# Attention plus feed-forward block: unpairing the last hidden chunk and retuning which engine takes which step

## The chip, the cores and the metric

The kernel runs on one core of a Trainium2 chip. A core has five engines with instruction streams of their own: TensorE (PE in the profile; its weight loads are listed apart as PEld), VectorE (DVE), ScalarE (ACT), GpSimd (POOL) and SyncE (SP), which here issues nearly all DMAs.[...] The metric is the device time of one execution in microseconds (us), lower is better. The time before is 734.32 us, the median of three runs (733.95 to 736.05).

## What is computed

The reference, cut to what matters (S = 2048 rows, D = 640, H = 32 query heads of 20, one shared key and value head, F = 1728):

```python
x  = A_x                                  # 1 x 2048 x 640, bf16
xn = (x - mean(x)) / sqrt(var(x) + 1e-5)
q  = (xn @ wq), split in 32 heads of 20;  k = xn @ wk;  v = xn @ wv
p  = softmax(q k^T / sqrt(20))            # 32 heads x 2048 x 2048
attention    = concat(p v) @ wo
feed_forward = silu(xn @ w1) @ w2         # 640 -> 1728 -> 640
out = x + attention + feed_forward
```

The costly part is the exponential of 32 x 2048 x 2048 scores, 134 million of them.

## The kernel before

The program is laid out by a list scheduler that runs when the kernel is built: every operation is given to an engine with a guessed duration, and the scheduler fixes each engine's order. On the chip an engine follows that order and waits where a semaphore has not come yet.

The scores are worked through in 128 units (4 chunks of 512 query columns x 32 heads), three units to a group, so 43 groups (the last holds two units). A group takes 16 steps, one for each 128 keys, so there are 688 steps. A step writes three PSUM banks of scores (S, one 512-column matmul for each unit). Then it has one of two shapes:

- In a **ScalarE step** one exponential of 128x1536 does all three banks.
- In a **VectorE step** ScalarE takes two banks (128x1024), and VectorE takes the third by integer arithmetic: it clips the score into an int16 (Z) whose bits are a coarse exponential. Two shifted copies of it, Y0 (VectorE) and Y1 (GpSimd), are read as well, so that the sum of three readings is an accurate exponential. The PV matmuls read all of them: Z and Y0 with the step itself, Y1 later, as a "third reading".

```python
def want_dve(self, t):                       # is step t a VectorE step?
    if t < DVE_FROM or ... or t % KT in KT_ACT:
        return False
    back = ...   # work that VectorE has in front of it, in the scheduler's us
    return back < DVE_TH
```

The PV matmuls of a step fill up to four column groups of 32 in one pass. A ScalarE step leaves one column group free and can carry a third reading in it; but the first step of a group cannot, because the fourth group has not been started there:

```python
        gd = self.group_dve[g]               # VectorE steps of this group so far
        pv.after = None if dv or nh < 3 or gd == 0 else thirds
...
    def emit_thirds(self, ts, first):        # (cut)
        for op, _ in self.pv_wait:           # ScalarE steps that can host a reading
            if seen and self.can_host(op) and ts:
                self.host(op, ts.pop())
        while len(self.thirds) >= 3 or (end and self.thirds):
            ...                              # the rest: passes of their own ("PT"), three readings each
```

After a group its sums (U) are copied to SBUF, turned by a DMA transpose, and normalised by GpSimd and VectorE. Behind the transpose of the first group stand the late weight loads on the same SyncE queue:

```python
    def norm_dma(self, g, rows):
        op = sc.dma("sp", lambda q: q.dma_start_transpose(self.UT[:, up, :, 0:rows], self.U[0:rows, up, :]), ...)
        if g == LATE_G:                      # group 0
            self.late_loads(("U", up))       # w2, wo, and a 1 MB fill of the query buffer
        ...                                  # GpSimd: two copies, two adds; VectorE: reciprocal; GpSimd: product
```

The feed-forward has 14 hidden chunks: 13 of 128 rows and one of 64. Each chunk of 512 columns gets 5 matmuls, a tanh on ScalarE and a product on VectorE (silu by way of tanh). The 64-row chunk is worked for two column chunks at once, in the two halves of the array's columns, with one tanh and one product over 128 partitions for both:

```python
    def h_job(self, c, fk, step):
        pair = fk == FC - 1
        ...
                for z in range(2):
                    ins = pe.matmul(self.bk(b, 0, QW, z * FLAST, (z + 1) * FLAST), self.w1[:, k, fk * P:fk * P + FLAST],
                                    self.xnT[:, k, (c + z) * QW:(c + z + 1) * QW], ..., tile_position=(0, z * FLAST))
        ...
            sc.new("act", t_act(QW), lambda a: a.activation(t, src, AF.Tanh, scale=0.5), ...)
            sc.new("dve", t_dve_ps(QW), lambda v: v.scalar_tensor_tensor(out=self.hT[0:rows, fk, :], ...), ...)
```

Jobs of the feed-forward's second half (14 matmuls of 320 columns for each of 32 output tiles, `out_job`) are put between the steps where the scheduler sees room. What is left when the last step is done runs in the tail, with the last attention output.

The prologue norms x (16 tiles): statistics by VectorE or ScalarE (`ACT_STATS` names ScalarE's tiles), an inverse square root for each batch of tiles (`BATCHES`, `NW_ENG`), the norm itself (`NORM_ENG`), and a transpose by DMA (`DT`) or TensorE. `PRO` is the order of TensorE's prologue jobs (t: transpose, k, q, v, d).

Of the kernel before, what the change touches and what calls it, by code (L numbers as in the profile page):

```python
# [14 lines left out]
P = 128  # L15
# [3 lines left out]
DC = 5  # L19
SLOT = 32  # L20
BANK = 512
QW = 512
# [5 lines left out]
FC = 14  # L28
FLAST = F - 13 * P
# [23 lines left out]
KT_ACT = (0,)  # L53
# [12 lines left out]
DVE_TH = 3.4  # L66
# [14 lines left out]
DT = (4, 5, 6, 9, 10, 11, 12, 13, 14, 15)  # L81
NORM_P = 4.5
DVE_FROM = 8
PRO = "v0 t7 t8 v1 k2 k3 k4 q1 v2 d0 k5 k6 k7 v3"
ACT_STATS = (4, 6, 9, 12, 14)
NW_ENG = ("dve", "dve", "dve")
NORM_ENG = ("pool", "pool", "pool", "pool", "act", "pool", "act", "act", "dve", "act", "act", "act")
BATCHES = ((0, 4), (4, 10), (10, 16))
# [256 lines left out]
class Job:  # L345
    def __init__(self, name, mms, reads, consume, gate=None, min_step=-1, banks=None, on_start=None, width=0, hold=None, use=None, n=1):
        self.name = name
        self.mms = mms
        self.reads = reads
        self.consume = consume  # L350
        self.gate = gate
        self.min_step = min_step
        self.on_start = on_start
        self.begun = False
        self.width = width
        self.hold = hold
        self.use = use
        self.n = n


class Builder:
# [371 lines left out]
    def do_mm(self, job, now, d):  # L733
        work, fn = job.mms.pop(0)
        job.begun = True
        b = job.bank
        op = self.sc.new("pe", d, lambda pe: fn(pe, b), job.reads, [("B", b)], name=job.name, queue=False)
        op.mm = job.n
# [353 lines left out]
    def h_job(self, c, fk, step):  # L1092
        sc = self.sc
        rows = P
        pair = fk == FC - 1
        mms = []
        for k in range(DC):
            def f(pe, b, k=k):
                if not pair:
                    return pe.matmul(self.bk(b), self.w1[:, k, fk * P:(fk + 1) * P], self.xnT[:, k, c * QW:(c + 1) * QW],  # L1100
                                     start=(k == 0), stop=(k == DC - 1))
                for z in range(2):
                    ins = pe.matmul(self.bk(b, 0, QW, z * FLAST, (z + 1) * FLAST), self.w1[:, k, fk * P:fk * P + FLAST],
                                    self.xnT[:, k, (c + z) * QW:(c + z + 1) * QW], start=(k == 0), stop=(k == DC - 1),
                                    tile_position=(0, z * FLAST), skip_group_check=True)
                return ins
            mms.append((t_mm(QW), f))
# [13 lines left out]
        reads = [("xnT", 4 * c + i) for i in range(8 if pair else 4)] + [("w1",)]  # L1121
        return Job(f"h{c}_{fk}", mms, reads, consume, min_step=step, width=0 if pair else QW, n=2 if pair else 1)
# [32 lines left out]
    def out_job(self, c, i, e, step=-1, ffn=True, ks=range(DC), src="xres", dst="ost", hmax=H):  # L1155
# [6 lines left out]
        if ffn:  # L1162
            for fk in range(FC):
                r0 = FLAST * (c % 2) if fk == FC - 1 else 0
                r1 = r0 + FLAST if fk == FC - 1 else P

                def f(pe, b, fk=fk, r0=r0, r1=r1, m=len(mms)):
                    return pe.matmul(self.bk(b, 0, 320), self.hT[r0:r1, fk, i * P:(i + 1) * P],  # L1168
                                     self.w2[r0:r1, fk, e0:e0 + 320], start=(m == 0), stop=(m == tot - 1))
                mms.append((t_mm(320), f))  # L1170
# [78 lines left out]
    def fill_chunk(self, c, t):  # L1249
# [11 lines left out]
        hs = [(3.0, lambda s, fk=fk: self.h_job(c, fk, s)) for fk in range(FC) if fk < FC - 1 or c % 2 == 0]  # L1261
# [46 lines left out]
    def prologue(self):  # L1308
# [41 lines left out]
        for fk in range(FC):  # L1350
            rows = P if fk < FC - 1 else FLAST
            for r0 in ((0,) if rows == P else (0, FLAST)):
                w2p.append(lambda q, fk=fk, rows=rows, r0=r0: q.dma_start(self.w2[r0:r0 + rows, fk, :],
                                                                          self.B_w2[fk * P:fk * P + rows, :]))
# [325 lines left out]
```

## Time and profile before

| | |
|---|---|
| median of three runs | 734.32 us |
| span of the profiled execution | 732.1 us |
| TensorE busy | 714.9 us (98%) |
| ScalarE busy | 695.8 us (95%) |
| VectorE busy | 652.6 us (89%) |
| GpSimd busy | 524.8 us (72%) |
| exponentials of 128x1536 / 128x1024 / 128x512 | 49 / 625 / 14 |
| tanh of 128x512 | 54 |
| VectorE steps | 637 of 688 |

The profile has one line for each group of like instructions: line of the kernel, engine, operation, what is written and read, the count, busy time and mean ns, and after the second bar how long the engine had stood idle before them and what ended the idle time. L776 is the score matmul, L794 the exponential, L808 VectorE's clip, L878 its Y0, L814 GpSimd's Y1, L866 all PV matmuls, L1100 and L1103 the hidden layer, L1113 tanh, L1118 the product, L1168 the feed-forward's second half, L956/L953/L958/L972 GpSimd's normalisation, L699/L712/L693 matmuls of zeros that fill gaps.

Engine time is counted as the union of intervals, and matmul and ScalarE intervals overlap their successors a little. So the distance from one start to the next, read from the timeline, is a better price for one more instruction than its duration.

### The profile page before, as it was taken

To read this page: it belongs to the slowest core of one execution; us is meant where nothing else is said; L and a number is where in the kernel's file an instruction comes from. 1 tells how busy PE (TensorE), PEld (TensorE's weight loads), DVE (VectorE), ACT (ScalarE), POOL (GpSimd) and SP (SyncE) were. 2 spreads that over 40 slices of the span, in tenths; PEclk is the share of its full clock that TensorE was granted. 3 is DMA by queue.
4 is the path that set the end of the run, shared out by engine and by line. 5 is a ranking of instruction groups with operands and counts; after the bars stand their busy time and mean duration, and the time that the engine had idled before them with its cause. 6 is when DMAs were issued, how large, how long until landed. Compare 5 with 4: busy or idle time off the path is not lost.

```text
span 732.1 us, 18886 instructions
## 1 busy us (share of the span) xinstructions
PE 714.9 (98%) x6863; PEld 229.2 (31%) x6863; DVE 652.6 (89%) x1189; ACT 695.8 (95%) x780; POOL 524.8 (72%) x897
## 2 busy tenths in 40 slices
PE   8898999999999999999999999999999999999998
PEld 4432222223333233222333233222233322322335
DVE  7788898998998999999899999999989899999883
ACT  6999999999999999999999999999999999999960
POOL 4376877677787777777777777767778877776770
PEclk9999999999999999999999999999999999999999
DMA  9546000000003011000102011110002001200011
GB/s 273 148 123 190 15 17 17 21 15 17 23 9 44 9 52 52 21 18 17 9 8 52 9 26 46 40 19 23 14 8 45 9 9 34 62 9 8 9 38 37
DMA packets 58546, 29.22 MB, mean 40 GB/s; under 512 B 44406, under 2 KB 57814, under 8 KB 58454
## 3 DMA queue, kind: packets, MB, share of 16 engines
q1 hardware_dynamic: 56998, 27.79, 15.1%
q8 instruction: 56, 0.92, 0.6%
q10 hardware_dynamic: 1456, 0.22, 0.2%
q14 instruction: 36, 0.29, 0.1%
HBM read 11.44 MB, written 2.62 MB: 19 GB/s over the span
## 4 chain that ended last, share of the span: by engine, by line
PE 70%; ACT 20%; issue 5%; DVE 4%; DMA 1%; POOL 1%; DVEq 0%; ACTq 0%; POOLq 0%
PE psall L866 23%; PE psall L776 22%; ACT sbt L794 18%; PE psall L1168 8%; PE psall L1100 7%; PE psall L1173 2%; PE psall L1064 2%; PE psall L712 2%; ACT sbt L1113 1%; DVE sbt L808 1%; PE psall L699 1%; DMA sbt<-sbt 1%; DVE sbt L1118 1%; ACT sbt L1458 1%; DVE sbt L1438 0%
## 5 line engine op out<-in xcount | busy, mean ns | idle before, releaser
L794 ACT ACTIVATE sbt<-psall 128x1024 bf16<-128x1024 f32 (+2 forms) x688 | 661.9, 1110 | 9.2 <-PE psall L776 7.7
L814 POOL TENSOR_TENSOR sbt<-sbt 128x256 int32<-128x256 int32 x637 | 436.8, 692 | 158.6 <-DVE sbt L808 143.9
L808 DVE TENSOR_SCALAR sbt<-psall 128x512 int16<-128x512 f32 x637 | 425.9, 684 | 48.2 <-PE psall L776 43.3
L776 PE MATMUL psall<-sbt 32*128 32x512 bf16 x2048 | 269.6, 385 | 6.4 <-ACT sbt L794 3.3
L866 PE MATMUL psall<-sbt 128*32 128x512 bf16 x3534 | 269.2, 385 | 2.1 <-POOL sbt L814 2.1
L776 PEld LDWEIGHTS psall<-sbt 32*128 32x128 bf16 x2048 | 69.2, 91 | 246.8 <-ACT sbt L794 81.1
L878 DVE TENSOR_SCALAR sbt<-sbt 128x1536 int16<-128x1536 int16 (+1 forms) x218 | 132.0, 608 | 2.0
L866 PEld LDWEIGHTS psall<-sbt 128*32 128x32 bf16 x3534 | 66.8, 94 | 113.7 <-issue 77.6
L1168 PE MATMUL psall<-sbt 128*128 128x320 bf16 x448 | 85.4, 302 | 0.2 <-DVE sbt L1118 0.2
L1100 PE MATMUL psall<-sbt 128*128 128x512 bf16 x260 | 79.9, 384 | 2.2 <-DVE sbt L1118 1.9
L1168 PEld LDWEIGHTS psall<-sbt 128*128 128x128 bf16 x448 | 34.7, 97 | 43.7 <-issue 33.1
L1118 DVE SCALAR_TENSOR_TENSOR sbt<-sbt,psall 128x512 bf16<-128x512 bf16 x54 | 36.8, 682 | 2.3 <-ACT sbt L1113 0.7
L1113 ACT ACTIVATE sbt<-psall 128x512 bf16<-128x512 f32 x54 | 37.1, 687 | 0.0
L986 DVE CAST sbt<-psall 128x512 bf16<-128x512 f32 x43 | 29.3, 682 | 1.7 <-PE psall L866 1.6
L1100 PEld LDWEIGHTS psall<-sbt 128*128 128x128 bf16 x260 | 17.8, 97 | 40.7 <-issue 25.8
L1064 PE MATMUL psall<-sbt 128*128 128x512 bf16 (+1 forms) x95 | 29.2, 385 | 0.4 <-DVE sbt L1118 0.4
L1173 PE MATMUL psall<-sbt 128*128 128x320 bf16 x144 | 29.0, 303 | 0.5 <-issue 0.4
L972 POOL TENSOR_TENSOR sbt<-sbt 128x240 bf16<-128x240 f32 (+2 forms) x44 | 25.4, 578 | 2.3 <-DMA sbt<-sbt 1.4
L958 POOL TENSOR_TENSOR sbt<-sbt 128x44 f32<-128x44 f32 x84 | 26.0, 309 | 1.1
L956 POOL CAST sbt<-sbt 128x168 f32<-128x168 bf16 x42 | 14.1, 335 | 9.0 <-DMA sbt<-sbt 9.0
L712 PE MATMUL psall<-sbt 128*128 128x512 bf16 (+1 forms) x70 | 17.4, 403 | 1.9 <-POOL sbt L1368 1.5
L1185 DVE SCALAR_TENSOR_TENSOR sbt<-psall,sbt 128x320 bf16<-128x320 f32 x28 | 13.6, 486 | 6.1 <-PE psall L1168 5.9
(88 smaller groups left out, 207.9 us busy)
## 6 DMA issues: line engine op xcount, KB each, us to landing
sbt<-in_A_x_dram SPq DMA_DIRECT2D x32, 160.0 KB, 3.3
out_dram<-sbt SPq DMA_DIRECT2D x15, 160.0 KB, 1.8
sbt<-in_B_w_dram SPq DMA_DIRECT2D x5, 432.0 KB, 6.6
sbt<-sbt SPq DMA_DIRECT2D x105, 20.0 KB
sbt<-in_B_w_dram SPq DMA_DIRECT2D x13, 160.0 KB, 2.9
sbt<-sbt SPq DMA_TRANSPOSE x68, 2.4
sbt<-sbt SPq DMA_DIRECT2D x1, 1024.0 KB, 6.1
sbt<-in_A_wo_dram SPq DMA_DIRECT2D x5, 160.0 KB, 2.7
```

The source lines that it names most:

```text
L776: ins = pe.matmul(self.bk(par3 + j), self.kT[r:r + SLOT, kk, kt * P:(kt + 1) * P], self.qT[r:r + SLOT, h // 4, (x // H) % 2, :], start=Tru ...
L794: return a.activation(self.E[:, b0 * QW:(b0 + na) * QW], self.ps[:, par3 * BANK:(par3 + na) * BANK], AF.Exp, scale=ACT_SCALE)
L808: return v.tensor_scalar(self.Z[:, zs, zp * QW:(zp + 1) * QW], self.bk(bb), 0.0, ZMAX, ALU.max, ALU.min)
L814: sc.new("pool", Y_TIME, lambda v: v.tensor_tensor(self.Y[:, zs, 1, zp * QW:(zp + 1) * QW].bitcast(I32), self.Z[:, zs, zp * QW:(zp + 1) * ...
L866: return pe.matmul(self.bk(UBANK, 0, QW, q * SLOT, (q + 1) * SLOT), self.v[:, w, kt, :], x, start=start, stop=stop, tile_position=(0, q * ...
L878: sc.new("dve", Y_SLOW + t_dve_4x(w), lambda v, k=k: v.tensor_scalar(self.Y[:, zs, k, 0:n * QW], Z, float(PH[k + 1][0]), None, ALU.add), z ...
L1064: return pe.matmul(self.bk(b, 0, QW, 0, rows), self.wq[:, k, lo:hi], self.xnT[:, k, c * QW:(c + 1) * QW], start=(k == 0), stop=(k == DC - 1))
L1100: return pe.matmul(self.bk(b), self.w1[:, k, fk * P:(fk + 1) * P], self.xnT[:, k, c * QW:(c + 1) * QW], start=(k == 0), stop=(k == DC - 1))
L1113: sc.new("act", t_act(QW), lambda a: a.activation(t, src, AF.Tanh, scale=0.5), [("B", b)], [("tb", tp)], prio=X_PRIO, name=f"th{c}_{fk}")
L1118: sc.new("dve", t_dve_ps(QW), lambda v: v.scalar_tensor_tensor(out=self.hT[0:rows, fk, :], in0=t, scalar=1.0, in1=src, op0=ALU.add, op1=AL ...
L1168: return pe.matmul(self.bk(b, 0, 320), self.hT[r0:r1, fk, i * P:(i + 1) * P], self.w2[r0:r1, fk, e0:e0 + 320], start=(m == 0), stop=(m == ...
L1173: return pe.matmul(self.bk(b, 0, 320), self.oT[:, k, i * P:(i + 1) * P], self.wo[:, k, e0:e0 + 320], start=(m == 0 and src != "ps"), stop= ...
```

## The change

It has four parts. The 64-row hidden chunk is no longer paired: each of the four column chunks does its own 64-row job, and the second copy of w2's last rows (in partitions 64 to 127) is no longer loaded. The rule that the first step of every group is a ScalarE step goes (`KT_ACT = ()`), and VectorE's permitted backlog is lowered (`DVE_TH` 3.4 to 2.6); so the backlog alone says where ScalarE steps fall, and they can fall inside a group, where they can carry a third reading, or end it. The prologue's assignment of work to engines is another one. The late loads stay behind the first group's U transpose. The purpose is a better balance between ScalarE, VectorE and TensorE, and a simpler hidden layer.

The diff (one cut, marked):

```diff
-KT_ACT = (0,)
+KT_ACT = ()
-DVE_TH = 3.4
+DVE_TH = 2.6
-DT = (4, 5, 6, 9, 10, 11, 12, 13, 14, 15)
-NORM_P = 4.5
+DT = (4, 5, 6, 7, 8, 9, 10, 12, 13, 14, 15)
+NORM_P = 0.5
-PRO = "v0 t7 t8 v1 k2 k3 k4 q1 v2 d0 k5 k6 k7 v3"
-ACT_STATS = (4, 6, 9, 12, 14)
-NW_ENG = ("dve", "dve", "dve")
-NORM_ENG = ("pool", "pool", "pool", "pool", "act", "pool", "act", "act", "dve", "act", "act", "act")
-BATCHES = ((0, 4), (4, 10), (10, 16))
+PRO = "v0 k2 t11 k3 v1 q1 k4 v2 d0 k5 k6 k7 v3"
+ACT_STATS = (2, 5, 6, 9, 10)
+NW_ENG = ("dve", "pool", "dve")
+NORM_ENG = ("pool", "pool", "pool", "act", "act", "dve", "act", "dve", "pool", "pool", "act", "act")
+BATCHES = ((0, 4), (4, 8), (8, 16))
     def h_job(self, c, fk, step):
-        rows = P
-        pair = fk == FC - 1
+        rows = P if fk < FC - 1 else FLAST
         for k in range(DC):
             def f(pe, b, k=k):
-                if not pair:
-                    return pe.matmul(self.bk(b), self.w1[:, k, fk * P:(fk + 1) * P], self.xnT[:, k, c * QW:(c + 1) * QW],
-                                     start=(k == 0), stop=(k == DC - 1))
-                for z in range(2):
-                    ins = pe.matmul(self.bk(b, 0, QW, z * FLAST, (z + 1) * FLAST), self.w1[:, k, fk * P:fk * P + FLAST],
-                                    self.xnT[:, k, (c + z) * QW:(c + z + 1) * QW], start=(k == 0), stop=(k == DC - 1),
-                                    tile_position=(0, z * FLAST), skip_group_check=True)
-                return ins
+                return pe.matmul(self.bk(b, 0, QW, 0, rows), self.w1[:, k, fk * P:fk * P + rows],
+                                 self.xnT[:, k, c * QW:(c + 1) * QW], start=(k == 0), stop=(k == DC - 1))
     def out_job(...)
-                r0 = FLAST * (c % 2) if fk == FC - 1 else 0
-                r1 = r0 + FLAST if fk == FC - 1 else P
-                    return pe.matmul(self.bk(b, 0, 320), self.hT[r0:r1, fk, i * P:(i + 1) * P],
-                                     self.w2[r0:r1, fk, e0:e0 + 320], start=(m == 0), stop=(m == tot - 1))
+                rows = P if fk < FC - 1 else FLAST
+                    return pe.matmul(self.bk(b, 0, 320), self.hT[0:rows, fk, i * P:(i + 1) * P],
+                                     self.w2[0:rows, fk, e0:e0 + 320], start=(m == 0), stop=(m == tot - 1))
     def fill_chunk(self, c, t):
-        hs = [(3.0, ... self.h_job(c, fk, s)) for fk in range(FC) if fk < FC - 1 or c % 2 == 0]
+        hs = [(3.0, ... self.h_job(c, fk, s)) for fk in range(FC)]
     def prologue(self):
-            for r0 in ((0,) if rows == P else (0, FLAST)):
-                w2p.append(... self.w2[r0:r0 + rows, fk, :] ...)
+            w2p.append(... self.w2[0:rows, fk, :] ...)
     (cut: the count of matmuls that a paired job told the scheduler)
```

## The prediction

> **What bounds the kernel now.** I read the shares of busy time first, then the busy time by stretches, then who waited for whom, and last the timeline of three places. In the stretches the columns are TensorE, its weight loads, VectorE, ScalarE and GpSimd, each with a count.
>
> ```profile
> PE 714.9 (98%) x6863; PEld 229.2 (31%) x6863; DVE 652.6 (89%) x1189; ACT 695.8 (95%) x780; POOL 524.8 (72%) x897
> ...
> 250.00:350.00 100.00, 99.47 (x954) 29.77 (x946) 93.02 (x161) 99.57 (x111) 73.17 (x124) 1.00 0.11 29
> ...
> PEld psall L776 <- ACT sbt L794: 81.1, 225, 0.8
> ...
> ACT sbt L1200 <- PE psall L1173: 17.6, 1, 17.6
> ACT sbt L794 <- PE psall L776: 7.7, 15, 2.0
> ```
>
> TensorE's 98% and ScalarE's 99.57 us of 100 cannot both be the bound. The waits decide: TensorE's weight loads for scores wait 81.1 us, 225 times, until an exponential has freed its banks, while the exponentials wait only 7.7 us for scores in the whole run. So from about 12 us to the last exponential near 710 us ScalarE is the bound, and a microsecond of work added to it is a microsecond of time. The 17.6 us is the tail, in which TensorE works alone.
>
> Two places break the rule. The first is a stall after the late loads:
>
> ```profile
> 62.60 2.12 SPq L943 DMA_TRANSPOSE sbt<-sbt  x1
> ...
> 68.89 0.33 POOL L956 CAST sbt<-sbt 128x168 f32<-128x168 bf16 x1 [3.26 <-DMA sbt<-sbt]
> ...
> 72.44 0.40 PE L866 MATMUL psall<-sbt 128*32 128x512 bf16 x4 [2.06 <-POOL sbt L814]
> ...
> 73.55 1.02 ACT L794 ACTIVATE sbt<-psall 128x1024 bf16<-128x1024 f32 x1 [2.04 <-PE psall L776]
> ```
>
> The second group's U transpose is issued at 62.60 behind the weight loads and lands at 68.8. GpSimd, whose order is fixed, stands 3.26 us in front of it; its Y1 for TensorE is late; TensorE then waits, and ScalarE loses 2.04 us. The second place is the tail on TensorE:
>
> ```profile
> 708.62 0.39 PE L776 MATMUL psall<-sbt 32*128 32x512 bf16 x2
> ...
> 710.31 1.69 PE L866 MATMUL psall<-sbt 128*32 128x512 bf16 x20
> ...
> 715.56 6.39 PE L1168 MATMUL psall<-sbt 128*128 128x320 bf16 x42
> ```
>
> After the last score at 708.62 there stand 65 feed-forward matmuls (2, 7, 14 and 42), 6.39/42 = 0.152 us each: work that had found no room earlier.
>
> **What the skill says.** "ScalarE: Activation LUTs", section "What ACT_TABLE_LOAD costs", gives an ACTIVATE with immediate operands 186 + 0.833 N ns, and an overlap of some 93 ns with the next one. The trace agrees with the first, 1090 ns for 128x1024 where the formula gives 1039; the overlap is about 0.19 us here (1.090 less the 0.903 below), twice the page's, and the trace's is used. "Perfetto Trace Analysis", section "Identifying the Most-Contended Engine", warns that TensorE's busy share does not tell how near it is to its limit; the 81.1 us above agree. "DMA: Bandwidth & Descriptors", section "Queues, rings and completion order", says that a DMA engine consumes the descriptors of one ring in their order; the U transpose that lands 6.2 us after its issue, where 2.4 us is the median of its kind, fits. "TensorEngine Tiling (Array Packing)", section "Key Properties", says that different tiles can run matmuls in parallel; in L1103, two matmuls in two column halves, 20 of them cover 3.1 us of busy time, or 0.31 us for a pair, and L1100's single ones 79.9/260 = 0.31. So the trace agrees, and unpairing doubles TensorE's passes.
>
> **Prices from the timeline**, start to start:
>
> ```profile
> 591.79 0.62 ACT L1113 ACTIVATE sbt<-psall 128x512 bf16<-128x512 f32 x1
> 592.27 6.56 ACT L794 ACTIVATE sbt<-psall 128x1024 bf16<-128x1024 f32 x7
> 598.59 0.72 ACT L1113 ACTIVATE sbt<-psall 128x512 bf16<-128x512 f32 x1
> ```
>
> A tanh costs 592.27 - 591.79 = 0.48 us, an exponential of 1024 (598.59 - 592.27)/7 = 0.903. One of 1536 took 1.33 (18.92 to 20.25), half a statistics pair 0.72 (18.20 to 18.92), a norm 0.82 (five in 4.17, the last one 0.91 long).
>
> **The change part by part.** The counts are from the order of instructions of the two built programs.
>
> 1. *ScalarE steps.* The exponentials go from 49 / 625 / 14 to 55 / 620 / 13 (1536 / 1024 / 512), with 630 VectorE steps in place of 637. That is 6 x 1.33 - 5 x 0.903 - 0.48 = +3.0 us, all on the bound.
> 2. *Unpairing.* Two tanh more, 2 x 0.48 = +1.0 us on the bound. Two more products on VectorE and 10 more passes on TensorE (5 for each of two jobs), at an estimate of 0.22 us each, are 2.2 us; they lie beside ScalarE's work.
> 3. *Third readings.* 47 are now carried by ScalarE steps inside their groups, none before. Passes of their own fall only from 213 to 207, as more groups end with a part-filled one. TensorE wins 6 x 0.22 = 1.3 us, so parts 2 and 3 together cost it about 1 us. It has 81 us of waits on ScalarE to put that in: no effect on the end.
> 4. *Prologue.* ScalarE still does five statistics pairs, but one more of them (tile 2) before the first TensorE transposes come back, where it stood idle 2.1 us. In the saturated stretch that saves 2 x 0.72 = 1.4 us, and one norm fewer saves 0.8. Against it, the first inverse square root now waits for ScalarE's statistics of tile 2; from the landing times I put that 0.3 us later. There are 11 DMA transposes in place of 10, at 14.55/10 = 1.46 us each in the queue, while ScalarE wants their keys earlier; I allow 0.2 us of waits. Together -1.7 us.
> 5. *The stall after the late loads.* Nothing is done about its cause but for one 80 KB load less (8.50/15 = 0.57 us of SyncE). GpSimd's order changes. Before, 29 Y1 precede the second group's first copy; now 26 do, so GpSimd comes to the same late transpose about three steps earlier and stands longer. In the order after, TensorE needs the Y1 of step 42 behind the scores of step 47; before, it needed that of step 41 behind step 45. From landing to the needed Y1 GpSimd took 72.4 - 68.9 = 3.5 us. Now it has two copies (0.3 each), six Y1 (0.61), two adds (0.25), a product (0.6) and three scalings of wo (0.73) in front of it, about 7.5 us. So 4.0 later, less the two steps at 0.9 us by which the need is later, less 0.57: the ScalarE stall grows from 2.0 by about 1.6 us.
> 6. *Tail.* After the last score the order has 52 feed-forward matmuls in place of 65: -13 x 0.152 = -2.0 us. There are 34 PV matmuls in place of 30, at 0.08 us each +0.3. The rest is alike. Sum -1.7 us.
>
> The sum: 3.0 + 1.0 - 1.7 + 1.6 - 1.7 = +2.2 us. I shade the stall term a little, because PV passes in front of the stalled one may fill in: +2.0, so 736.3 us.
>
> **Rivals.**
>
> *TensorE is the true bound.* Its 98% and the feed-forward work left over for the tail speak for it. Then the 10 passes count, the saved passes count, and the tail's smaller remainder is only work moved forward: about +1 us net for TensorE, without ScalarE's +2.3 (parts 1, 2 and 4) and without the tail's gain, 735.3 us. The 81 us of waits on ScalarE speak against it.
>
> *VectorE is relieved and the steps run smoother.* Seven VectorE steps fewer and a lower backlog could shorten the 45.2 us that score loads waited for VectorE's clip; TensorE reads its third readings later (on average 7.8 steps behind instead of 6.8). If that mattered, the time could fall to 732 us. But ScalarE is idle only about 0.4 us in 100, so there is hardly anything to win outside the stall.
>
> *The stall disappears.* If the transpose lands early enough (one load less, the other order on GpSimd), ScalarE gains the 2.0 us instead of losing 1.6: 736.3 - 3.6 = 732.7 us. Against it: the loads in front of it are the same 4 MB less 2%.
>
> *The new prologue does not hold its keys.* An 11th transpose pushes the last key block back by 1.46 us while ScalarE wants it some 2 us sooner; if the slack before was below that, ScalarE loses up to 3 us: 739.3 us. The small waits of before (0.26 and 0.44 us around 37 us) say that some slack was left.
>
> **Range and chances.** Parts 1, 2 and 6 are counts by measured prices and should hold within 0.5 us each. The two stalls are uncertain by some 2 us each, mostly upwards. This gives 733.5 to 739.5 us. Two per cent are 14.7 us, six times the expected sum; nothing in the list is near it. So faster 0.01, same 0.96, slower 0.03.
>
> **What would show each step right or wrong.** ScalarE's busy time should rise by about 3.2 us (3.0 + 1.0 - 0.8, the statistics being only moved), with prices unchanged. The first copy of the second group on GpSimd should wait about 5 us instead of 3.26, and one exponential between 65 and 80 us should wait 3 to 4 us for scores. The stretch from the last score to the end should shrink from 23.5 to 21.8 us. TensorE's waits on exponentials should stay near 80 us; if they fall to a fraction while the exponentials begin to wait, the first rival is right. The prediction is wrong if the stall is absent, or if many exponentials outside it wait for scores.

## The result, and the profile after

The changed kernel takes **741.86 us** (median of four runs, 741.56 to 742.66) against 734.66 for the kernel before, measured beside it. The ratio is 1.0097, with a 95% interval of 1.0080 to 1.0115: slower by about 7.2 us, within the 2% that the prediction gave nearly all its chances to. But the time lies outside the predicted range of 733.5 to 739.5, and 5.6 us above the predicted 736.3. The profiled execution spans 740.2 us (732.1 before).

The shares of busy time, the busy times from 250 to 350 us, and the waits, in the order of those shown of before:

```profile
PE 718.4 (97%) x6816; PEld 228.4 (31%) x6816; DVE 654.2 (88%) x1177; ACT 699.5 (95%) x781; POOL 523.3 (71%) x902
```

```profile
250.00:350.00 100.00, 98.99 (x943) 28.42 (x941) 93.24 (x161) 99.78 (x111) 72.58 (x126) 1.00 0.11 31
```

```profile
PEld psall L774 <- ACT sbt L792: 81.8, 210, 1.0
...
ACT sbt L1190 <- PE psall L1163: 15.9, 1, 15.9
...
ACT sbt L792 <- PE psall L774: 14.5, 15, 4.4
```

From 250 to 350 us nothing has changed: ScalarE is busy 99.78 us of 100. Over the whole run TensorE's weight loads wait for exponentials as long as before (81.8 us, 81.1 before). ScalarE's busy time rose by 3.7 us, its wait for the tail fell from 17.6 to 15.9. What is new is the third line: the exponentials' waits for scores have nearly doubled, from 7.7 to 14.5 us, in as many waits. So few long waits have grown. The timeline of ScalarE shows two of them early; first the changed kernel, then the kernel before:

```profile
38.48 3.77 ACT L792 ACTIVATE sbt<-psall 128x1024 bf16<-128x1024 f32 x4 [3.13 <-PE psall L774]
43.74 6.95 ACT L792 ACTIVATE sbt<-psall 128x1024 bf16<-128x1024 f32 x7 [1.49 <-PE psall L774]
```

```profile
36.99 1.02 ACT L794 ACTIVATE sbt<-psall 128x1024 bf16<-128x1024 f32 x1 [0.26 <-PE psall L776]
38.46 33.05 ACT L794 ACTIVATE sbt<-psall 128x1024 bf16<-128x1024 f32 x35 [0.44 <-PE psall L866]
```

Together 3.13 + 1.49 = 4.62 us, where before had 0.26 + 0.44 = 0.70. And here is the place of the late loads, all engines, from the second group's U transpose on:

```profile
65.59 2.02 SPq L941 DMA_TRANSPOSE sbt<-sbt  x1
...
72.32 0.33 POOL L954 CAST sbt<-sbt 128x168 f32<-128x168 bf16 x1 [5.79 <-DMA sbt<-sbt]
...
74.27 0.26 POOL L956 TENSOR_TENSOR sbt<-sbt 128x40 f32<-128x40 f32 x1
...
74.57 0.23 DVE L961 RECIPROCAL sbt<-sbt 128x12 f32<-128x12 f32 x1 [5.10 <-POOL sbt L956]
...
74.71 1.22 DVE L806 TENSOR_SCALAR sbt<-psall 128x512 int16<-128x512 f32 x2
...
75.40 0.61 PE L774 MATMUL psall<-sbt 32*128 32x512 bf16 x3 [4.40 <-DVE sbt L806]
...
76.11 1.02 ACT L792 ACTIVATE sbt<-psall 128x1024 bf16<-128x1024 f32 x1 [4.40 <-PE psall L774]
```

Read from below: the exponential waits 4.40 us for scores, the scores for a clip that frees their bank, the clip stands in VectorE's order behind the second group's reciprocal, which waits 5.10 us for GpSimd, which waits 5.79 us for the transpose behind the bulk loads. With 0.42, 0.98, 0.16 and 0.16 us that follow, ScalarE loses 6.1 us here; before it lost 2.04 + 0.76 + 0.21 = 3.0. Last, TensorE's timeline after the last score:

```profile
718.31 0.39 PE L774 MATMUL psall<-sbt 32*128 32x512 bf16 x2
...
721.03 0.58 PE L1158 MATMUL psall<-sbt 128*128 128x320 bf16 x3
...
722.08 1.23 PE L1158 MATMUL psall<-sbt 128*128 128x320 bf16 x7
...
723.37 2.17 PE L1158 MATMUL psall<-sbt 128*128 128x320 bf16 x14
...
725.71 4.28 PE L1158 MATMUL psall<-sbt 128*128 128x320 bf16 x28
```

52 feed-forward matmuls (3 + 7 + 14 + 28), as predicted, and 740.2 - 718.3 = 21.9 us to the end.

So the account of the 8.1 us between the two spans is: ScalarE busy +3.7, key waits near 40 us +3.9, late-load waits near 76 us +3.1, tail -1.7, the rest (above all shorter waits of ScalarE in the prologue) -0.9.

### The profile page after: what moved, and what is told of

It reads as the page before. It is cut to its first block, busy times and chain, and to the rows that moved or that the text cites. A ratio compares the mean times of both kernels' runs of the same rounds, so it can differ in the third digit from the quotient of the medians.

```text
span 740.2 us, 18787 instructions
## 1 busy us (share of the span) xinstructions
PE 718.4 (97%) x6816; PEld 228.4 (31%) x6816; DVE 654.2 (88%) x1177; ACT 699.5 (95%) x781; POOL 523.3 (71%) x902
## 4 chain that ended last, share of the span: by engine, by line
PE 72%; ACT 18%; issue 4%; DVE 3%; POOL 1%; DMA 1%; DVEq 0%; ACTq 0%; POOLq 0%
PE psall L864 24%; PE psall L774 23%; ACT sbt L792 15%; PE psall L1158 9%; PE psall L1096 8%; PE psall L1163 3%; PE psall L1062 2%; DVE sbt L806 2%; PE psall L711 2%; ACT sbt L1104 2%; DMA sbt<-sbt 1%; PE psall L698 1%; POOL sbt L812 1%; ACT sbt L1447 1%; DVE sbt L876 0%
## 5 line engine op out<-in xcount | busy, mean ns | idle before, releaser
L792 ACT ACTIVATE sbt<-psall 128x1024 bf16<-128x1024 f32 (+2 forms) x688 | 665.5, 1104 | 16.1 <-PE psall L774 14.5
L864 PE MATMUL psall<-sbt 128*32 128x512 bf16 x3482 | 267.3, 385 | 0.3 <-DVE sbt L984 0.2
L774 PEld LDWEIGHTS psall<-sbt 32*128 32x128 bf16 x2048 | 69.1, 91 | 260.4 <-ACT sbt L792 81.8
L876 DVE TENSOR_SCALAR sbt<-sbt 128x1536 int16<-128x1536 int16 (+2 forms) x220 | 131.7, 600 | 3.3
L864 PEld LDWEIGHTS psall<-sbt 128*32 128x32 bf16 x3482 | 65.9, 94 | 110.5 <-issue 74.5
L1096 PE MATMUL psall<-sbt 128*128 128x512 bf16 (+1 forms) x280 | 85.0, 385 | 0.3 <-DVE sbt L1109 0.2
L1158 PEld LDWEIGHTS psall<-sbt 128*128 128x128 bf16 x448 | 34.4, 97 | 43.6 <-issue 33.2
L1109 DVE SCALAR_TENSOR_TENSOR sbt<-sbt,psall 128x512 bf16<-128x512 bf16 (+1 forms) x56 | 38.2, 681 | 6.3 <-ACT sbt L1104 3.3
L1104 ACT ACTIVATE sbt<-psall 128x512 bf16<-128x512 f32 (+1 forms) x56 | 38.0, 679 | 0.0
L1096 PEld LDWEIGHTS psall<-sbt 128*128 128x128 bf16 (+1 forms) x280 | 19.1, 98 | 40.7 <-issue 29.7
L1062 PE MATMUL psall<-sbt 128*128 128x512 bf16 (+1 forms) x95 | 29.0, 385 | 0.2
L711 PE MATMUL psall<-sbt 128*128 128x512 bf16 (+2 forms) x84 | 22.2, 406 | 1.4 <-POOL sbt L1357 1.4
L1175 DVE SCALAR_TENSOR_TENSOR sbt<-psall,sbt 128x320 bf16<-128x320 f32 x28 | 13.6, 487 | 5.3 <-PE psall L1158 4.8
```

What stands on the lines that cost most here:

```text
L774: ins = pe.matmul(self.bk(par3 + j), self.kT[r:r + SLOT, kk, kt * P:(kt + 1) * P], self.qT[r:r + SLOT, h // 4, (x // H) % 2, :], start=Tru ...
L792: return a.activation(self.E[:, b0 * QW:(b0 + na) * QW], self.ps[:, par3 * BANK:(par3 + na) * BANK], AF.Exp, scale=ACT_SCALE)
L864: return pe.matmul(self.bk(UBANK, 0, QW, q * SLOT, (q + 1) * SLOT), self.v[:, w, kt, :], x, start=start, stop=stop, tile_position=(0, q * ...
L876: sc.new("dve", Y_SLOW + t_dve_4x(w), lambda v, k=k: v.tensor_scalar(self.Y[:, zs, k, 0:n * QW], Z, float(PH[k + 1][0]), None, ALU.add), z ...
L1062: return pe.matmul(self.bk(b, 0, QW, 0, rows), self.wq[:, k, lo:hi], self.xnT[:, k, c * QW:(c + 1) * QW], start=(k == 0), stop=(k == DC - 1))
L1096: return pe.matmul(self.bk(b, 0, QW, 0, rows), self.w1[:, k, fk * P:fk * P + rows], self.xnT[:, k, c * QW:(c + 1) * QW], start=(k == 0), s ...
```

## The experiments

Theory A after this reading: two waits carry the surprise, one for key blocks that the new prologue brings too late, one for the transpose behind the late loads. Rivals: the new step rule disturbs all steps a little; TensorE, not ScalarE, is the bound; the prologue change costs in some other way. Runs made together share a chip and the runs of before; across them I compare ratios to before, and a gain or loss in us is the ratio's share of 734 us. "Spread" below means a version in which the late loads are not issued in one block.

| run | what it is | median, us | ratio to before (95%) |
|---|---|---|---|
| e1_prologue | before, the change's prologue | 739.71 | 1.0071 (1.0050 to 1.0093) |
| e2_steps | before, the change's step rule | 738.98 | 1.0062 (1.0043 to 1.0081) |
| e3_unpair | before, hidden chunk unpaired | 738.54 | 1.0052 (1.0035 to 1.0068) |
| e4_old_prologue | changed, prologue of before | 745.76 | 1.0154 (1.0135 to 1.0174) |
| e5_t78 | changed, tiles 7 and 8 turned by TensorE | 740.91 | 1.0086 (1.0065 to 1.0108) |
| e6_spread | changed, spread | 734.82 | 1.0007 (0.9994 to 1.0021) |
| e7_known | changed, order planned for the late landing | 738.77 | 1.0060 (1.0038 to 1.0081) |
| e8_t78_spread | e5 and spread | 734.12 | 0.9995 (0.9986 to 1.0005) |
| e9_before_spread | before, spread | 728.81 | 0.9919 (0.9888 to 0.9949) |
| e10_old_prologue_spread | e4 and spread | 736.49 | 1.0029 (1.0016 to 1.0043) |
| e11_e2_spread | e2 and spread | 731.44 | 0.9960 (0.9946 to 0.9975) |
| e12_d0_spread | e8, query projection behind the keys | 739.52 | 1.0063 (1.0048 to 1.0078) |
| e13_d0_first | e8, query projection early | 739.62 | 1.0079 (1.0066 to 1.0091) |
| e14_before_d0_first | before, spread, prologue of e13 | 731.43 | 0.9960 (0.9946 to 0.9974) |
| e15_prologue_spread | before, spread, the change's prologue | 729.44 | 0.9947 (0.9933 to 0.9960) |
| e16_before_spread_again | e9 again | 727.75 | 0.9918 (0.9904 to 0.9931) |

### Each part alone

**e1_prologue**: the seven prologue settings of the change (`DT` to `BATCHES` in its diff) in the kernel before.

> The kernel before with the prologue settings of the change alone (DT, NORM_P, PRO, ACT_STATS, NW_ENG, NORM_ENG, BATCHES). Theory A, late arrivals: the 5.5 us that I missed are waits of ScalarE for the last key blocks (near 38 and 43 us) and behind the second group's U transpose (near 75 us), and the prologue causes the first. Then the first wait returns in full (3.1 + 1.5 us near 40 us), ScalarE saves 1.4 + 0.8 us of statistics and norm, the tail has 85 in place of 90 feed-forward matmuls (-0.8), and the second wait grows by 1 to 2 us: 736.5 to 738 us. Rival B, the loss lies in the steady part (where ScalarE steps fall, and the unpaired chunk): the prologue alone costs nothing, 731.5 to 733.5 us.

It is +5.2 us by its ratio, more than either expected. ScalarE is busy 1.0 us less (694.8), but its waits for scores rise from 7.7 to 15.1 us: 3.11 + 1.87 near 40 us and 5.2 near 77 us. So the prologue alone makes both waits of the changed kernel: the first directly, the second probably because the first U transpose goes out at 55.09 us in place of 49.21 and takes the late loads with it.

**e2_steps**: the step rule.

```diff
-KT_ACT = (0,)
-DVE_TH = 3.4
+KT_ACT = ()
+DVE_TH = 2.6
```

> The kernel before with the step rule of the change alone (KT_ACT empty, DVE_TH 2.6). Its order has 63 / 611 / 14 exponentials of 1536 / 1024 / 512 in place of 49 / 625 / 14 and 55 in place of 90 feed-forward matmuls after the last score. Theory A: ScalarE +14 x 0.427 = +6.0 us, tail -35 x 0.152 = -5.3 us, wait behind the U transpose +1 to 2 us because GpSimd and VectorE come to it two to three steps earlier, no wait near 40 us: 735.5 to 737.5 us. Rival B: steps placed inside groups disturb the steady part too, with many small waits of exponentials between 100 and 650 us: over 739 us. Rival C, TensorE is the true bound: fewer passes and a shorter tail win, 730 to 732 us.

+4.6 us, above theory A's range. ScalarE is busy 7.4 us more (703.2), its wait for the tail is 4.6 us shorter (13.0), and the waits near 76 us come to 6.3 us where before had 3.0; near 38 us there are only 0.50. So the rule, too, lengthens the late-load wait by itself, probably by moving the orders of GpSimd and VectorE around the transpose (its reciprocal waits 4.39 us), and the steady part stays undisturbed: the small-waits rival falls.

**e3_unpair**: the hidden chunk alone (`h_job`, `out_job`, `fill_chunk` and the w2 load of the diff).

> The kernel before with the 64-row hidden chunk unpaired alone. Its order has two tanh more and 118 in place of 90 feed-forward matmuls after the last score. Theory A: ScalarE +1.0 us, tail +28 x 0.152 = +4.3 us and 0.5 us for six more PV matmuls, the wait behind the U transpose 0 to 1 us more: 740 to 742 us. If the ten passes were hidden beside ScalarE, as I predicted for the change: 735.7 us.

+3.8 us; the median of 738.54 lies below theory A's 740 to 742 and well above the 735.7 of hidden passes. Its waits, to be set beside 81.1, 17.6 and 7.7 us of before:

```profile
PEld psall L774 <- ACT sbt L792: 94.9, 256, 0.8
...
ACT sbt L1190 <- PE psall L1163: 22.3, 1, 22.3
...
ACT sbt L792 <- PE psall L774: 5.9, 13, 1.8
```

The exponentials wait less than before, but the tail is 4.7 us longer. Behind the last score the trace has 94 feed-forward matmuls (5 + 7 + 12 + 70) in place of 66, and 28 x 0.152 = 4.3 us. (The expectations count by the built order, which gives 24 more: 118 and 90.) So with the ten passes that I called hidden, the order leaves 28 more matmuls for the tail, where nothing hides them. TensorE's waits for exponentials did not shrink, they rose to 94.9 us: room that the chip shows is used only if the scheduler, which plans with guessed durations, puts work there.

**e4_old_prologue**: the changed kernel with the prologue of before.

> The changed kernel with the prologue settings of before. 60 / 613 / 15 exponentials, 94 feed-forward matmuls after the last score (76 in the changed kernel). Theory A: the wait of 4.6 us near 40 us goes and 0.7 us come back, ScalarE pays 2.2 us more for statistics and norm and 1.3 us for three more ScalarE steps, the tail +18 x 0.152 = +2.7 us, the wait near 75 us becomes about 1.5 us shorter: 742 to 743.5 us, about the time of the changed kernel, but with the loss in the tail and not near 40 us. Rival B: undoing the prologue brings nothing back and costs nothing in the tail, 741 to 742 us with waits in the steady part.

It became slower, by 0.57% (1.0154 against 1.0097, 4.2 us), above both expected ranges. The key wait went as expected (0.19 + 0.50 us near 37), but the late-load wait stayed (4.85 and three small ones, 6.2 us in all), ScalarE is busy 2.3 us more and the tail is 2.2 us longer. So the three parts don't add: alone they cost 5.2 + 4.6 + 3.8 = 13.6 us, together 7.2, and taking the prologue back makes the changed kernel slower.

### The wait behind the late loads

**e6_spread** (in short): the changed kernel, the fill of the query buffer behind the first U transpose, then three pieces of w2 and wo behind each of the next ones.

```diff
-        if g == LATE_G:
+        if g >= LATE_G:
             self.late_loads(("U", up))
...
+        todo = [fill] + w2_pieces + wo_pieces
         def late_loads(key):
-            load_w2([key]); load_wo([key]); fill([key])
+            for f in todo[:1 if g == LATE_G else 3]: f([key]); todo.remove(f)
```

> The changed kernel with the late loads spread out: the 1 MB fill of the query buffer behind the first group's U transpose as before, then three pieces of w2 or wo (160 KB each) behind each of the following groups' transposes. Nothing else is edited; its order has 54 / 621 / 13 exponentials, the same tail. Theory A: the wait of ScalarE near 75 us (6.1 us in pieces) is the landing of the second U transpose behind 3 MB of loads; with one fill before it, it lands some 8 us earlier and the wait ends: 735 to 736.5 us, with the 4.6 us near 40 us still there. Rival: the wait comes from VectorE's and GpSimd's order (the reciprocal in front of the clips) whatever the landing: 740 us or more.

734.82 us: 1.0007 in place of 1.0097, about 6.6 us won. The second U transpose of this kernel:

```profile
63.18 1.21 SPq L941 DMA_TRANSPOSE sbt<-sbt  x1
...
67.35 0.33 POOL L954 CAST sbt<-sbt 128x168 f32<-128x168 bf16 x1 [0.96 <-DMA sbt<-sbt]
...
72.05 0.22 DVE L961 RECIPROCAL sbt<-sbt 128x12 f32<-128x12 f32 x1
```

GpSimd waits 0.96 us in place of 5.79, the reciprocal not at all, and ScalarE has no wait there. The Trainium skill, "DMA: Bandwidth & Descriptors", section "Queues, rings and completion order", says that descriptors are consumed in the order of their ring. This run agrees: with the bulk loads taken from in front of it, the transpose is used 4.2 us after its issue in place of 6.7.

**e7_known**: the changed kernel with its loads in one block, but the scheduler told that a U transpose lands behind the transfers before it, so that it puts the second group's normalisation later in the orders of GpSimd and VectorE.

```diff
-            if op.name in ("oTd", "xTd", "uTd"):
+            if op.name in ("oTd", "xTd"):
                 self.dma_t = op.end
-            op.avail = op.end + 1.6 if op.name in ("oTd", "xTd", "uTd") else max(op.end + 2.0, ...)
+            op.avail = op.end + 1.6 if op.name in ("oTd", "xTd") else max(op.end + (1.6 if uTd else 2.0), ...)
```

> The changed kernel, its scheduler told that a U transpose lands behind the loads in front of it (two lines in its landing rule; the loads stay where they are). GpSimd then comes to the second group's first copy after 35 in place of 26 Y1, and VectorE puts its reciprocal eleven clips later. 61 / 614 / 13 exponentials. Theory A: the transpose lands as late as before, but nobody stands in front of it: the 6.1 us go to under 1.5 us, ScalarE pays 6 x 0.427 = 2.6 us for six more ScalarE steps: 738.5 to 740 us. If the late landing itself holds up the work (U's two buffers), the wait stays and the time is over 743 us.

738.77 us, as expected. The transpose is as late, but no engine stands in front of it: one wait of 0.44 us is left. So here the late landing by itself cost ScalarE next to nothing; what cost was an in-order engine that had other work and stood in front of it. The other planning spent some of the gain (ScalarE busy 2.1 us more).

**e9_before_spread**: the same spreading on the kernel before.

> The kernel before with its late loads spread (the fill behind the first U transpose, three pieces of w2 or wo behind each of the following ones); exponentials stay at 49 / 625 / 14, and the order of instructions leaves 57 feed-forward matmuls to run after the last score where before leaves 90. Theory A (ScalarE bounds the steps, TensorE has room for that work): the waits near 70 to 77 us (3.0 us) go and the tail loses 33 x 0.152 = 5.0 us, so about 726 us, 725 to 729. Theory B (TensorE's budget is as full as ScalarE's, so the 33 matmuls moved forward are paid as waits of ScalarE): only the 3.0 us of the stall, 730 to 732.5 us, with more waits of the exponentials in the steps.

728.81 us, 0.9919; the best so far, at the upper end of theory A's range. One of TensorE's lines:

```profile
37.14 0.27 PE L1584 MATMUL psall<-sbt 128*128 128x256 bf16 x1 [1.34 <-DMA sbt<-sbt]
```

The wait for the tail fell from 17.6 to 13.2 us, 4.4 of the 5.0 us that A expected, and near 77 us nothing waits. In this execution the last key block waited 1.34 us for a transpose of x, and ScalarE 2.75 us near 40. In **e16_before_spread_again**, the same program, that was gone:

> Before with spread loads again (728.8 us in its first run), for the comparison with the other three on the same chip: 727 to 730 us, ratio to before 0.990 to 0.995. In its first profile the last key block waited 1.34 us for a DMA transpose; if that belongs to the program and not to one execution, it shows again.

727.75 us, ratio 0.9918, near 38 us only 0.25 + 0.43. Theory A stands for these matmuls: moved from the tail into the steps they cost ScalarE at most 0.6 us. Its waits for scores are 5.3 us in all, where before had 7.7 with the 3.0 of the stall.

**e11_e2_spread**: the step rule of e2 with spread loads.

> Before with the new rule for ScalarE steps and with spread loads, the hidden chunk still paired: exponentials 56 / 618 / 14, 48 feed-forward matmuls after the last score. Against the same rule without spread loads (739.0): the waits near 76 us go (-6.3), the tail has 7 matmuls fewer (-1.1): about 731.6, 730.5 to 733. If it is also faster than before with spread loads, the new rule has a worth of its own; theory A says it hasn't, as its 7 more wide exponentials cost +3.0 and it saves only 9 x 0.152 = 1.4 in the tail.

731.44, as expected, but 0.41% (3.0 us) above e9 and 0.42% above e16, whose interval (0.9904 to 0.9931) lies below its own: the rule by itself is a loss.

**e10_old_prologue_spread**: the changed kernel with both waits taken away, by the prologue of before and by spreading.

> The changed kernel with the prologue of before and with spread loads: neither of the two waits that I blame should be left. Against the changed kernel with spread loads alone (734.8): waits near 40 us -3.9, ScalarE's prologue work back +1.7, exponentials 57 / 617 / 14 in place of 54 / 621 / 13 = 3 x 1.33 - 4 x 0.903 + 0.48 = +0.9, 8 feed-forward matmuls more in the tail +1.2: about 734.7, 733.5 to 736. That would say that the change's other parts gain nothing over before once both waits are gone. If the prologue had a hidden worth, it would be slower than 736.5.

736.49, a little above the range; the waits are as small as expected (0.20 + 0.50 near 38, 0.42 near 83), and ScalarE stood 3.0 us in front of the first transposes (2.15 before; one program shows 1.67 in e9 and 2.38 in e16). Against e11, which differs by the unpairing alone, it is 0.69% (5.1 us) slower: 60 feed-forward matmuls in the tail by the trace in place of 24, 36 x 0.152 = 5.5 us. So even without either wait the change does not gain: its step rule costs 3.0 and its unpairing 5.1 us.

### The wait for the keys

TensorE's timeline of the changed kernel, at the last three key blocks (L1556; L1069 is the evacuation of the query projection for later heads, L1566 GpSimd's copy of a key block):

```profile
36.16 1.26 PE L1556 MATMUL psall<-sbt 128*128 128x256 bf16 x10 [0.98 <-DVE sbt L1069]
37.98 0.61 PE L774 MATMUL psall<-sbt 32*128 32x512 bf16 x6 [0.55 <-POOL sbt L1566]
...
43.30 0.61 PE L774 MATMUL psall<-sbt 32*128 32x512 bf16 x6 [1.03 <-POOL sbt L1566]
```

The same in the kernel before (L1567 and L1577 there):

```profile
34.13 0.94 PE L1567 MATMUL psall<-sbt 128*128 128x256 bf16 x7
...
36.50 0.39 PE L776 MATMUL psall<-sbt 32*128 32x512 bf16 x3 [0.56 <-POOL sbt L1577]
```

There the blocks begin at 34.13 us, 2 us sooner, while ScalarE gets to its fifth exponential 1.5 us later (29.48 for 28.02). No wait of TensorE between 30 and 44 us of the changed kernel ends on a DMA, so it isn't the landing of the transposes of x that holds these blocks.

**e5_t78**: the 11 DMA transposes back to 10. If the extra one delays the keys, this cures them.

```diff
-DT = (4, 5, 6, 7, 8, 9, 10, 12, 13, 14, 15)
-PRO = "v0 k2 t11 k3 v1 q1 k4 v2 d0 k5 k6 k7 v3"
+DT = (4, 5, 6, 9, 10, 11, 12, 13, 14, 15)
+PRO = "v0 t7 t8 v1 k2 k3 k4 q1 v2 d0 k5 k6 k7 v3"
```

> The changed kernel with only the list of transposes of before: tiles 7 and 8 turned by TensorE instead of tile 11 (DT and PRO of before). Theory A: the wait near 40 us starts with tile 9, whose DMA transpose is the sixth in the queue in the changed kernel and the fourth before; key block 4 waits for it, and the jobs behind it in TensorE's fixed order (v2, d0, k5, k6, k7) with it. Then ScalarE's 4.6 us there fall to about 1 us, the wait near 75 us stays at 5 to 6 us: 737.5 to 739 us. Rival: what is late is the order itself (k5 and k6 stand behind the q job d0 in both), or the slow square root on GpSimd: then it stays at 741 to 742 us.

740.91, and the waits are 0.33 + 2.52 + 1.45 = 4.3 in place of 4.6 us. That theory fell: the transposes' number is not the cause. In e4, which differs from this run only in `NORM_P`, `ACT_STATS`, `NW_ENG`, `NORM_ENG` and `BATCHES`, the key waits were 0.69 us. So with the old transposes and order it is these five settings that bring the wait. They say what engine takes the statistics, the inverse square roots and the norms, and in what batches. **e8_t78_spread** joins it with the spreading:

> e5 and e6 together. Theory A: both waits go, 741.9 - 3.6 - 6.5 = 731 to 733.5 us, faster than the kernel before. If the two waits hide one another (the second only moves work that the first had delayed), the gains do not add: 734.5 us or more.

734.12; it missed for the same reason, the key waits are there:

```profile
28.18 7.31 ACT L792 ACTIVATE sbt<-psall 128x1536 bf16<-128x1536 f32 x6 [0.34 <-PE psall L774]
...
38.04 3.77 ACT L792 ACTIVATE sbt<-psall 128x1024 bf16<-128x1024 f32 x4 [2.56 <-PE psall L774]
43.31 18.38 ACT L792 ACTIVATE sbt<-psall 128x1024 bf16<-128x1024 f32 x19 [1.50 <-PE psall L774]
```

They sum to 4.40 us. e10, which again differs by the five settings alone, has 0.20 + 0.50. e10 is slower than e8 all the same (1.0029 against 0.9995): ScalarE is busy 2.2 us more (700.6 for 698.4) and waits 0.9 us longer for the tail (16.6 for 15.7).

**e12_d0_spread**: the query projection behind the keys in the prologue of e8.

```diff
-PRO = "v0 t7 t8 v1 k2 k3 k4 q1 v2 d0 k5 k6 k7 v3"
+PRO = "v0 t7 t8 v1 k2 k3 k4 q1 v2 k5 k6 k7 d0 v3"
```

> The changed kernel with spread loads and with the transposes of tiles 7 and 8 on TensorE (734.1 us), and the projection of queries for later heads moved in TensorE's prologue from in front of the last three key blocks to behind them. Theory A (the keys are late because those five matmuls and their evacuation on VectorE stand in front of them): the exponentials' waits between 36 and 45 us (0.34 + 2.56 + 1.50 = 4.4) fall to 0.3 to 1.5 us. Theory B (ScalarE simply gets there before the transposes of x have landed): they stay at 3.5 or above. The scheduler also makes other steps ScalarE steps: exponentials 61 / 613 / 14 in place of 54 / 621 / 13, 7 x 1.33 - 8 x 0.903 + 0.48 = +2.6, and 8 more matmuls in the tail, +1.2; so the time stays near 734.4 by A, 737.5 by B.

The waits are 0.34 us at 28.5, 1.64 at 38.4 and 1.44 at 42.7, 3.4 in all, close to theory B's 3.5. The step that had waited 2.56 us now has its scores 2.2 us sooner (35.34 for 37.55) and doesn't wait; the next one does (1.64), for PV passes (L864) that TensorE does only behind the scores of step 12, and these for another key block. The time is 739.52, 5.4 us above e8. The profiled span is 4.2 us longer, and that is ScalarE's other work: it is busy 3.2 us more (701.6 for 698.4, as the scheduler makes more steps ScalarE steps) and waits 0.8 us longer for the tail (16.56 for 15.74). The rest lies outside the span, and no trace explains it.

**e13_d0_first** and **e14_before_d0_first**: the projection early instead, in the changed kernel and in the kernel before, both with spread loads.

```diff
-PRO = "v0 t7 t8 v1 k2 k3 k4 q1 v2 d0 k5 k6 k7 v3"
+PRO = "v0 t7 t8 v1 d0 k2 k3 k4 q1 v2 k5 k6 k7 v3"
```

> The changed kernel with spread loads and tiles 7 and 8 transposed on TensorE (734.1 us), the query projection for later heads moved in front of all key blocks but the first two; in TensorE's order the last three key blocks now stand behind steps 7 to 10 and the PV passes in front of step 12. Theory A (order: each key block needs its matmuls, VectorE's cast and GpSimd's copy, and TensorE and VectorE had put other work in front of them): waits between 36 and 45 us fall from 4.4 to 1 us or less. Theory B (the transposes of x land too late for the earlier ScalarE): 3 us or more stay. Exponentials 57 / 617 / 14 (+0.9) and 8 more matmuls in the tail (+1.2): 732.8 us by A, 735.5 by B.

> Before with spread loads and with the change's prologue, tiles 7 and 8 on TensorE and the query projection first. Exponentials and tail are those of before with spread loads (49 / 625 / 14, 57 matmuls). Theory A: no key waits above 1 us, ScalarE's 1.7 to 2 us of saved prologue work come through: 727 us, the fastest so far. Theory B: 3 us of key waits eat it: 729.5 to 730.5.

Both missed (739.62 and 731.43), and the order theory with them. ScalarE's longest waits in e14 are 2.38 us at 29.7 and 2.45 us at 45.7. They stand in front of an earlier step and of a later one; with the four between them they sum to 7.0 us, in place of 5.0 in e15. e13's span is 5.6 us longer than e8's: ScalarE is busy 2.1 us more (700.5), waits 2.5 us more for scores (11.2 for 8.7) and 0.8 more for the tail. In these three runs moving the one job only moved the place where ScalarE waits.

**e15_prologue_spread** is the clean pair for the prologue: it and e16 have the same exponentials (49 / 625 / 14), the same 33 matmuls in the tail by the trace, and no late-load wait.

> Before with spread loads and with the change's prologue as it is. Only the prologue differs from the next run. By the trace of the changed kernel it saves ScalarE about 2 us and waits 3.9 us longer for keys: +1.5 to +2.5 us against that run, with waits of 4 to 5 us between 36 and 45 us and none near 77 us. Rival: the prologue's cost in the run of it alone (+5.4 us) was all its own: +4.5 to +5.5.

729.44 against 727.75, +1.7 us, as expected. First e15, then e16, ScalarE's waits from 36 to 46 us:

```profile
39.10 3.77 ACT L794 ACTIVATE sbt<-psall 128x1024 bf16<-128x1024 f32 x4 [3.14 <-PE psall L776]
44.77 19.32 ACT L794 ACTIVATE sbt<-psall 128x1024 bf16<-128x1024 f32 x20 [1.90 <-PE psall L776]
```

```profile
37.68 1.02 ACT L794 ACTIVATE sbt<-psall 128x1024 bf16<-128x1024 f32 x1 [0.25 <-PE psall L776]
39.14 19.88 ACT L794 ACTIVATE sbt<-psall 128x1024 bf16<-128x1024 f32 x21 [0.43 <-PE psall L866]
```

5.04 us for 0.68. ScalarE's saving is more than handed back, and the 5.2 us that the prologue cost in e1 were this and the late-load wait that it lengthens.

## Why the prediction was wrong

Its step 4 failed: it allowed the key blocks 0.2 us of waits, and they took 3.9 us more. Its step 5 was mis-sized, 3.1 us for 1.6. The other terms of the sum held.

1. *Steps 1 and 2, ScalarE's work* (+3.0, +1.0 less the prologue's 0.8): ScalarE's busy time rose by 3.7 us where 3.2 was predicted. Right.
2. *Steps 2 and 3, TensorE's passes* ("no effect on the end"): wrong as a rule, as e3 (+3.8 us) and the pair e10 and e11 (+5.1) show. The price of 0.22 us a pass was sound: at 32.62 us of the kernel before, five matmuls of 512 columns take 1.25 us, each 0.38 long, so (1.25 - 0.38)/4 = 0.22. It did not spoil the sum, because step 6 read the tail's matmuls from the order itself.
3. *Step 4, the prologue* ("I allow 0.2 us of waits. Together -1.7 us"): its saving was right. From the first exponential to the fifth, ScalarE took 28.02 - 17.48 = 10.54 us where before took 29.48 - 16.86 = 12.62, a saving of 2.1 for the predicted 2.2, and the first exponential came 0.6 us later for the predicted 0.3. (The idle time that the moved statistics were to fill is still there, 2.02 us for 2.15, and a difference of 0.6 us is within what the first exponential varies, as the last section shows.) But the key waits grew by 3.9 us and not by 0.2. So the term is 0.6 - 2.1 + 3.9 = +2.4 in place of -1.7, 4.1 us off; the clean pair e15 and e16 puts the whole prologue at +1.7. In the changed kernel this term isn't what one wins by taking the prologue back: in e4 the key waits go and the kernel is 4.2 us slower, because the scheduler then makes another order. The rival "the new prologue does not hold its keys" named the right wait, with up to 3 us, but not its mechanism. It blamed an 11th transpose at 1.46 us; e5 takes that away, and 4.3 of the 4.6 us stay. The 1.46 was a misreading besides: the stretch of 14.55 us holds waits between the issues, the median issue is 1.28 us, and the eleven of the changed kernel take 14.57. I had also taken two small waits of 0.26 and 0.44 us as a sign of slack. The first of them says the opposite: the scores at 36.50 us had waited 0.56 us for GpSimd's copy of a key block, so there the keys already set the time.
4. *Step 5, the late loads* ("from 2.0 by about 1.6 us"): the growth was 3.1 us, from 3.0 to 6.1 with the small waits that follow. The root was right (GpSimd's first copy waited 5.79 us, predicted about 5; e6 and e7 took it away), the path was another. I followed GpSimd's Y1 to TensorE. In the changed order it was VectorE that stood in front of its reciprocal (5.10 us, 1.88 before) with the clips behind it, and a clip frees the score banks at once. I had also left out that the first U transpose starts 4.4 us later (53.58 for 49.21), with everything behind it.
5. *Step 6, the tail* (-1.7): 17.6 to 15.9 us, and 21.9 us from the last score where 21.8 was predicted. Right, though the trace of before has 66 matmuls there and not 65: one more starts at 708.94.

None of the prediction's other rivals came true: TensorE's weight loads still wait 81.8 us for exponentials, their waits for VectorE's clip rose from 45.2 to 51.0 us, and the stall grew.

With 4.1 us for the prologue and 1.5 for the loads the predicted +2.2 becomes +7.8, which is near what the spans (+8.1) and the medians (+7.2) show. That the five settings of statistics, norms and batches bring the key waits is shown twice (e4 and e5, e10 and e8). By what path they do it is **not settled**. It isn't the number of DMA transposes (e5), nor the query projection in front of the key blocks alone (e12 to e14). In the timelines each block is a chain of short pieces (5 matmuls, a cast of 0.41 us on VectorE, a copy of 0.48 us on GpSimd) with waits between them, and the orders of three engines would have to be shifted together to test it; that stays open.

The version that beats both kernels is e16: the kernel before with its late loads spread, 727.75 us, 0.9918 (0.9904 to 0.9931). Neither the prologue nor the step rule improves it (e15, e11).

## What to carry to other kernels

A microsecond saved on the bound engine counts only up to that engine's next wait: before booking it, find what that wait ends on, and whether that comes sooner too; a small wait there can mean that nothing is left to give. An in-order engine placed in front of a transfer that queues behind bulk loads hands its wait to everything placed behind it, so bulk loads go out in pieces or the consumer goes later. Work that looks hidden beside a bound engine can come out at the end, so count what the schedule leaves for the tail.

## What the runs showed beyond that

The same prologue begins its exponentials at different times in different kernels and executions: 16.59 us (e4), 16.77 (e9), 16.86 (before), 17.47 (e16, the program of e9), 17.85 (e10), 17.96 (e11), 18.17 (e3). That is more than the effects of some parts, and a single profile of the prologue should be read with it in mind. Within one program an x transpose landed late enough to hold a key block by 1.34 us in one execution (e9) and not in another (e16).
